# A fused attention and spectral-mixing kernel: v on the software DMA queue, a regrouped tail, and one SyncE transfer per stored pair

## The chip, the cores and the metric

The kernel runs on one core of a Trainium2 chip, in one launch. The metric is the device time in microseconds (us); medians are quoted. The record marks each run as fast or slow. All runs of kernels that were timed more than once are marked fast (none is over 1.5% above the fastest of its kernel); for the five single runs (e5 to e8 and e11) the state is unknown. A profile is one execution taken by the hardware profiler. Its span is about 2 us shorter than the time that is measured for the same execution (460.2 against 461.99 us for the kernel before).

PE is the matrix engine, PEld its weight loads, DVE the vector engine, ACT the scalar engine, POOL and SP (SyncE) the two engines that issue the DMA transfers here. Transfers from POOL go to the software DMA queue (q0), those from SyncE to the hardware queue (q1). Sixteen DMA engines serve both. Every operation is recorded through one helper, so all profile lines carry its line number, L37, and are told apart by the names of their tiles.

## The reference, cut to what matters

```python
# q, k, v: [8, 8, 576, 64] f32; w_phi: [64, 128]
# moe_w_r, moe_w_i: [64, 512, 512] f32 (134 MB together); moe_w_ch: [512, 512]
q_p, k_p = phi(q), phi(k)                 # t = x @ w_phi - max|x @ w_phi|; exp(t), exp(-t)
x = (q_p @ (k_p^T v)) / (q_p @ sum(k_p))  # heads side by side: [8, 576, 512]
X = rfft(x, axis=1)[:, :64]               # 64 modes
Y = per mode, complex: X[:, m] @ (w_r[m] + i w_i[m])
u = x + irfft(Y, n=576)
out = u + relu(u @ moe_w_ch)              # [8, 576, 512] f32, 9.44 MB
```

The kernel makes the attention per pair of batches and pair of heads, while the 64 weight tiles of the modes (2 MB of f32 each in HBM, cast to bf16 on the way) stream in behind. As the inverse transform and the product with `w_ch` are both linear, it keeps the mixed modes Y ("y") and Y @ w_ch ("z") and adds the inverse transform of y to x, and that of z to x @ w_ch. A "mix" is the product of modes with one weight tile. yst and zst are the tiles that hold the y and z of the modes just mixed, and yT is yst transposed. The first 48 modes are "absorbed" into x and x @ w_ch before the last weights are there; the other 16 ("late") are added in the tail, chunk by chunk, where the relu, the last sum and the store of the output follow.

## The kernel before

These are the parts that the change and the argument touch. A chunk is 128 rows of the output in SBUF: chunks 0 to 7 of a batch pair come in pairs (n, n + 1). In a pair's output tile, partition 64a + p holds rows 9p + 4a + c and 9p + 4a + c + 1 of one batch. Chunk 8 holds one row in nine of both batches.

```python
def load_v(self):
    self.vn = pin.tile([128, 2, 9, D_], F32, name="vn")
    load(self.vn, v, self.g, self.bp, sp)              # SyncE
...
class Absorb:                                          # y and z of one chunk
    def sums(self):
        r = slice(0, 96)
        self.p, self.q = bank(), bank()                # two PSUM banks
        back(self.p, self.n, self.bp, CI, yall, r)
        pe.matmul(self.q, lhsT=ident_b, rhs=xw[:, self.bp, self.n, :], ...)
        back(self.q, self.n, self.bp, CI, zall, r)
    def keep_x(self): ...                              # DVE: x += p
    def keep_w(self): ...                              # ACT: xw = q
...
# after each mix of the last group of weights (cut): the serial chain
    dve.tensor_tensor(out=yst, in0=py, in1=yacc[:, o, :], op=ALU.add)
    put(yst, o, yall, (0, 2))
    ...                                                # 4 transposes
    act.copy(yT, pt)
    ...                                                # 4 matmuls of 512 columns
    act.copy(zst, pz)
    put(zst, o, zall, (1, 3))
    # three absorbs (ab[-3], ab[-2], ab[-1]) lie between these steps at the very end
...
class Last:                                            # the tail, a pair of chunks
    def store(self):
        rows = [out[2 * bp + i].rearrange("(p c) e -> p c e", c=9) for i in range(2)]
        if n == 8:
            ...                                        # two halves: (sp, pool)
        o = pw.tile([128, 2, DMODEL], F32, name="of", tag="wt")
        dve.tensor_tensor(out=o, in0=self.pp, in1=self.rl, op=ALU.add)
        i, c = n // 4, n % 4
        for a in range(2):
            (sp, pool)[a].dma_start(
                rows[i][:, 4 * a + c:4 * a + c + 2, :], o[64 * a:64 * a + 64])
```

## Time and profile before

| | before |
|---|---|
| time, median of 3 runs | 462.84 us (461.55 to 462.95) |
| span of the profiled run | 460.2 us |
| HBM read, written | 163.64 MB, 9.44 MB |
| last mix begins | 416.42 us |
| first store issued | 426.27 us |
| stores | 40 transfers of 64 partitions, 20 from SyncE, 20 from POOL |

These two rows of the page cut the span into 40 slices of 11.5 us: the mean busy share of the 16 DMA engines (in tenths, 9 is 90% or more), and what they moved.

```profile
DMA  8999999999999999999999999999999999992897
GB/s 192 207 216 220 230 229 209 228 229 207 229 230 209 228 229 227 209 230 229 207 229 228 207 207 207 206 208 207 207 213 218 214 211 211 205 178 55 249 323 252
```

The DMA engines are busy from the second slice to the 36th, that is until about 414 us, then idle for one slice, then busy again with the stores. Everything up to the gap is paced by the loads, most of which are weights.

In the windows view each row is a stretch of time: its length, the busy us of each engine with the number of instructions, the granted clock of PE (1.00 is full speed), the DMA share and the GB/s moved. A share above 1 means that packets overlap.

```profile
core 0: us, PE busy (x) PEld busy (x) DVE busy (x) ACT busy (x) POOL busy (x), PEclk, DMA share, GB/s
...
400.00:410.00 10.00, 9.87 (x55) 3.63 (x56) 7.06 (x11) 6.59 (x12) 0.00 (x0) 1.00 1.37 206
410.00:414.00 4.00, 4.00 (x25) 1.65 (x25) 3.02 (x6) 2.85 (x5) 0.00 (x0) 1.00 0.80 133
414.00:417.00 3.00, 1.33 (x12) 0.49 (x10) 1.04 (x2) 1.24 (x3) 0.00 (x0) 1.00 0.22 36
...
428.00:440.00 12.00, 12.00 (x68) 3.59 (x65) 9.87 (x10) 8.58 (x16) 4.78 (x9) 1.00 0.97 315
440.00:452.00 12.00, 10.51 (x61) 3.17 (x60) 10.35 (x10) 7.92 (x15) 4.76 (x9) 1.00 0.92 304
```

The timeline (start, duration, engine, operation, count, idle time before it and what ended that) shows the chain between:

```profile
416.42 0.67 PE L37 MATMUL pt<-wt,XT 128*32 128x512 bf16 x8 [1.67 <-DMA wt<-in_moe_w_i_dram]
...
417.13 0.69 DVE L37 TENSOR_TENSOR yst<-pt,yacc 128x512 bf16<-128x512 f32 x1 [2.09 <-PE pt L37]
...
420.13 0.58 ACT L37 CAST zst<-pt 128x512 bf16<-128x512 f32 x1 [0.68 <-ACT xw L37]
...
425.01 1.23 DVE L37 TENSOR_TENSOR of<-pp,rl 128x1024 f32<-128x1024 f32 x1 [3.90 <-PE pp L37]
...
426.27 5.25 SPq L37 DMA_DIRECT2D out_dram<-of  x4
...
451.04 0.68 DVE L37 TENSOR_TENSOR ofr<-pp,rl 128x512 f32<-128x512 f32 x1
...
454.95 1.67 SPq L37 DMA_DIRECT2D out_dram<-ofr  x1
```

PE waits 1.67 us for the last weight tile. Its product goes through yst, the transposes, zst and the first sums to the first pair add (425.01), and the first store goes out at 426.27. The last store leaves SyncE at 454.95, although DVE had finished it at 451.72: SyncE's queue is behind. The DMA view lists the transfers of v and of the output: issuing engine, count, KB each, median us from issue to landing.

```profile
vn<-in_v_dram SPq DMA_DIRECT2D x16, 576.0 KB, 7.8
...
out_dram<-of SPq DMA_DIRECT2D x16, 256.0 KB, 4.9
out_dram<-of POOLq DMA_DIRECT2D x16, 256.0 KB, 5.0
...
out_dram<-ofr SPq DMA_DIRECT2D x4, 128.0 KB, 5.0
out_dram<-ofr POOLq DMA_DIRECT2D x4, 128.0 KB, 4.8
```

`of` is the output tile of a pair, `ofr` that of chunk 8.

### The profile page before, as it was taken

How to read it: one execution, taken by the hardware profiler on the slowest of the kernel's cores; microseconds unless marked ns; L12 is line 12 of the kernel's file. 1: busy time of each engine (PE TensorE's matmuls, PEld its weight loads, DVE VectorE, ACT ScalarE, POOL GpSimd, SP SyncE). 2: the span in 40 equal slices, each digit the busy share in tenths (PEclk: the TensorE clock that was granted, in tenths of full speed). 3: DMA queues.
4: the chain of work that ended last, by engine and by line, in shares of the span. 5: the costliest groups of instructions: out<-in, count | busy, mean ns of one | idle time of the engine just before them, and what ended most of it. 6: DMA issues, size and time to landing. Idle time of an engine off the chain costs nothing.

```text
span 460.2 us, 9716 instructions
## 1 busy us (share of the span) xinstructions
PE 331.6 (72%) x4041; PEld 207.1 (45%) x4084; DVE 270.0 (59%) x488; ACT 281.6 (61%) x475; POOL 92.4 (20%) x130
## 2 busy tenths in 40 slices
PE   1586767768767767877866776059997756997991
PEld 1365546546555545655654554024443322332330
DVE  6656676556677658568647784643331213773882
ACT  3696879676889769579758762214452322664771
POOL 6232112113111211222110115002121210000331
PEclk9998999797999999789879999559998987999997
DMA  8999999999999999999999999999999999992897
GB/s 192 207 216 220 230 229 209 228 229 207 229 230 209 228 229 227 209 230 229 207 229 228 207 207 207 206 208 207 207 213 218 214 211 211 205 178 55 249 323 252
DMA packets 86301, 99.27 MB, mean 216 GB/s; under 512 B 2800, under 2 KB 79728, under 8 KB 86256
## 3 DMA queue, kind: packets, MB, share of 16 engines
q0 software_dynamic: 77264, 81.80, 103.8%
q1 hardware_dynamic: 8992, 16.85, 12.0%
q8 instruction: 32, 0.52, 0.4%
q14 instruction: 13, 0.11, 0.1%
HBM read 163.64 MB, written 9.44 MB: 376 GB/s over the span
## 4 chain that ended last, share of the span: by engine, by line
issue 27%; PE 23%; ACT 15%; DMA 15%; DVE 13%; POOL 5%; POOLq 0%; ACTq 0%
PE one L37 9%; PE pt L37 8%; DMA wt<-in_moe_w_i_dram 7%; PE two L37 6%; DVE m L37 6%; DMA kb<-in_k_dram 6%; ACT AB L37 5%; ACT AQ L37 5%; DVE mk L37 2%; POOL wt L37 2%; POOL out_dram L37 2%; DMA qb<-in_q_dram 2%; DVE zall L37 2%; ACT kT L37 2%; ACT XT L37 1%
## 5 line engine op out<-in xcount | busy, mean ns | idle before, releaser
L37 ACT CAST xw<-pt 128x512 bf16<-128x512 f32 x72 | 42.0, 586 | 61.7 <-PE pt L37 60.5
L37 ACT ACTIVATE AB<-two 128x1024 bf16<-128x1024 f32 x64 | 62.8, 1051 | 6.2 <-DVE mk L37 3.8
L37 ACT ACTIVATE AQ<-two 128x1024 bf16<-128x1024 f32 x64 | 63.0, 1053 | 1.9 <-PE two L37 1.8
L37 PE MATMUL pt<-wchb,xT 128*128 128x512 bf16 x135 | 39.8, 412 | 20.0 <-DVE xT L37 19.7
L37 DVE TENSOR_REDUCE m<-two 128x8 f32<-128x1024 f32 x32 | 39.2, 1224 | 17.8 <-PE two L37 17.7
L37 DVE TENSOR_REDUCE mk<-two 128x8 f32<-128x1024 f32 x32 | 39.0, 1221 | 16.7 <-PE two L37 16.3
L37 POOL DMA_DIRECT2D wt<-in_moe_w_r_dram x30 | 26.3, 878 | 95.7 <-PE one L37 52.9
L37 POOL DMA_DIRECT2D wt<-in_moe_w_i_dram x28 | 24.5, 876 | 91.0 <-PE pt L37 46.1
L37 DVE TENSOR_TENSOR va<-vn,ee 128x1152 bf16<-128x1152 f32 x32 | 42.0, 1356 | 0.0
L37 DVE RECIPROCAL rd<-one 128x6 f32<-128x6 f32 x48 | 9.4, 195 | 51.5 <-PE one L37 51.5
L37 ACT COPY kT<-one 128x512 bf16<-128x512 bf16 (+1 forms) x32 | 19.2, 640 | 28.7 <-PE one L37 28.7
L37 DVE TENSOR_TENSOR xs<-pt,xs 128x512 bf16<-128x512 f32 x36 | 24.3, 691 | 19.0 <-PE pt L37 18.6
L37 PEld LDWEIGHTS <-minus 96*128 96x128 bf16 x288 | 26.3, 110 | 19.0 <-issue 13.4
L37 PEld LDWEIGHTS <-XT 128*32 128x32 bf16 x512 | 17.9, 180 | 34.2 <-issue 21.6
L37 PE MATMUL two<-w2blk,qT 128*128 128x256 bf16 x128 | 20.4, 285 | 17.6 <-ACT AB L37 12.9
L37 DVE COPY xT<-pt 128x512 bf16<-128x512 bf16 x36 | 15.1, 422 | 30.3 <-PE pt L37 30.3
L37 PE MATMUL two<-mT,minus 96*128 96x128 bf16 x256 | 29.3, 245 | 3.1 <-issue 1.9
L37 PEld LDWEIGHTS <-xs 128*128 128x128 bf16 x304 | 24.7, 100 | 15.2 <-issue 8.1
L37 POOL DMA_DIRECT2D kb<-in_k_dram x16 | 11.5, 716 | 95.5 <-PE one L37 94.7
L37 PEld LDWEIGHTS <-qT 128*128 128x128 bf16 x144 | 14.1, 101 | 32.5 <-issue 29.9
L37 PE MATMUL one<-kvz,AQ 128*128 128x65 bf16 x512 | 28.0, 211 | 0.0
L37 DVE TENSOR_TENSOR xs<-one,rd 128x384 bf16<-128x384 f32 x48 | 26.8, 558 | 1.6
(113 smaller groups left out, 673.9 us busy)
## 6 DMA issues: line engine op xcount, KB each, us to landing
wt<-in_moe_w_r_dram POOLq DMA_DIRECT2D x30, 1024.0 KB, 28.1
wt<-in_moe_w_i_dram POOLq DMA_DIRECT2D x28, 1024.0 KB, 28.6
vn<-in_v_dram SPq DMA_DIRECT2D x16, 576.0 KB, 7.8
kb<-in_k_dram POOLq DMA_DIRECT2D x16, 288.0 KB, 22.3
qb<-in_q_dram POOLq DMA_DIRECT2D x16, 288.0 KB, 22.1
out_dram<-of SPq DMA_DIRECT2D x16, 256.0 KB, 4.9
out_dram<-of POOLq DMA_DIRECT2D x16, 256.0 KB, 5.0
xs<-in_moe_w_i_dram POOLq DMA_DIRECT2D x2, 1024.0 KB, 26.9
```

Of the source, the lines that this page charges most:

```text
L37: ins = f(*args, **kwargs)
```

## The change: its intent, and the diff

The change means to shorten the tail and to free the hardware queue. v is loaded from POOL. In the tail, the first two chunks are finished one by one in PSUM banks of their own; for the first four chunks the absorbing of y goes ahead of that of z; yst, yT, z's product and zst are made in halves shared between DVE and ACT; all absorbs are done before the last mix. Each stored pair goes out in one SyncE transfer in place of two of 64 partitions. Cut to its core:

```diff
-            load(self.vn, v, self.g, self.bp, sp)
+            load(self.vn, v, self.g, self.bp, pool)
...
-    todo += [c.all for c in ab[:-3]]
+    todo += [c.only_x for c in ab[:4]] + [c.only_w for c in ab[:4]] + [c.all for c in ab[4:]]
...
-            dve.tensor_tensor(out=yst, in0=py, in1=yacc[:, o, :], op=ALU.add)
+            for h in range(2):
+                dve.tensor_tensor(out=yst[:, H * h:H * h + H], in0=py[:, H * h:H * h + H],
+                                  in1=yacc[:, o, H * h:H * h + H], op=ALU.add)
...
-            act.copy(zst, pz)
+            act.copy(zst[:, 0:H], pz[0])
+            dve.tensor_copy(zst[:, H:], pz[1])
...
-            for a in range(2):
-                (sp, pool)[a].dma_start(
-                    rows[i][:, 4 * a + c:4 * a + c + 2, :], o[64 * a:64 * a + 64])
+            rows = out[2 * bp + n // 4]
+            sp.dma_start(
+                bass.AP(tensor=rows.tensor, offset=rows.offset + n % 4 * DMODEL,
+                        ap=[[4 * DMODEL, 2], [9 * DMODEL, 64], [1, w * DMODEL]]),
+                o.rearrange("p a e -> p (a e)") if w > 1 else o)
...
     seq = [Last(bp, ns) for bp in range(NP) for ns in ((0, 1), (2, 3), (4, 5), (6, 7), (8,))]
+    seq[0:1] = [Last(0, (0,)), Last(0, (1,))]
```

The list `ap` gives [step, count] per dimension of the output side, slowest first: 2 x 64 x (512w), w being 2 for a pair and 1 for the first two chunks. The two outer dimensions cannot be merged, as 64 steps of 9 rows are not one step of 4 rows. The SBUF side of the same transfer counts 128 partitions. Chunk 8 is also stored in one SyncE transfer, but there 128 partitions stand against 128 equally spaced rows.

More of the change, by code (lines that the diff above doesn't have):

```diff
@@ L543, with banks @@
     ps2_cm.__exit__(None, None, None)
-    pst_cm = tc.tile_pool(name="pst", bufs=8, space=bass.MemoryType.PSUM)
-    pst = pst_cm.__enter__()
+    pst = ctx.enter_context(tc.tile_pool(name="pst", bufs=4, space=bass.MemoryType.PSUM))
+    pst2 = ctx.enter_context(tc.tile_pool(name="pst2", bufs=2, space=bass.MemoryType.PSUM))
     def bank(shape=(128, DMODEL), dt=F32):
         return pst.tile(list(shape), dt, name="pt", tag="pt")
+    def banks(dt=F32):
+        return pst2.tile([128, 2, DMODEL * (1 if dt == F32 else 2)], dt, name="pp", tag="pp")
     pb_cm = tc.tile_pool(name="pb", bufs=2)
@@ L557 @@
     CL = pb.tile([128, 5, 128], BF16, name="CL", bufs=1)
-    CM = pb.tile([128, 4, 128], BF16, name="CM", bufs=1)
+    CM = CF.rearrange("p c r m -> p (c r m)")[:, 0:1024].rearrange(
+        "p (i c s) -> p i c s", i=2, c=4)
     def inverse_tables():
@@ L595, in inverse_tables @@
         last = calc(calc(tm, 4.0, jm), 1.0, 56.0)
-        b0 = calc(b0, 0.0, 1.0, ALU.is_equal, ALU.mult)
-        for dst, m, r, only in ((CI, mode, r, None), (CL, late, r, None), (CM, last, rm, b0)):
+        b0, b1 = (calc(b0, float(i), 1.0, ALU.is_equal, ALU.mult) for i in range(2))
+        for dst, m, r, only in ((CI, mode, r, None), (CL, late, r, None), (CM[:, 0], last, rm, b0),
+                                (CM[:, 1], last, rm, b1)):
             n = 512 if only is not None else 640
@@ L650, in __init__, with sum_p, sum_q @@
             self.bp, self.n = bp, n
-        def sums(self):
-            r = slice(0, 96)
-            self.p, self.q = bank(), bank()
-            back(self.p, self.n, self.bp, CI, yall, r)
-            pe.matmul(self.q, lhsT=ident_b, rhs=xw[:, self.bp, self.n, :],
-                      start=True, stop=False)
-            back(self.q, self.n, self.bp, CI, zall, r)
+        def sum_p(self, p):
+            self.p = p
+            back(p, self.n, self.bp, CI, yall, slice(0, 96))
+        def sum_q(self, q):
+            self.q = q
+            pe.matmul(q, lhsT=ident_b, rhs=xw[:, self.bp, self.n, :], start=True, stop=False)
+            back(q, self.n, self.bp, CI, zall, slice(0, 96))
         def keep_x(self):
@@ L666, in keep_w, with only_x, only_w @@
             act.copy(xw[:, self.bp, self.n, :], self.q)
-        def all(self):
-            self.sums()
+        def only_x(self):
+            self.sum_p(bank())
+            self.keep_x()
+        def only_w(self):
+            self.sum_q(bank())
+            self.keep_w()
+        def all(self):
+            if chunks.index((self.bp, self.n)) % 2:
+                p, q = bank(), bank()
+            else:
+                t = banks()
+                p, q = t[:, 0], t[:, 1]
+            self.sum_p(p)
+            self.sum_q(q)
             self.keep_x()
@@ L686 @@
     ab = [Absorb(*c) for c in chunks]
-    todo += [c.all for c in ab[:-3]]
+    todo += [c.only_x for c in ab[:4]] + [c.only_w for c in ab[:4]] + [c.all for c in ab[4:]]
+    A = len(ab) + 4
     def fill(n):
@@ L699, in put @@
                 r = 32 * s + 16 * (o - 6)
-                sp.dma_start(yl[r:r + 16], src)
+                (sp, pool)[s // 2 if o == 7 else 0].dma_start(yl[r:r + 16], src)
     todo = [inverse_tables] + todo
-    while mixq:
-        key = mixq.pop(0)
-        g, o, i = key[0], key[1] // 2, key[1] % 2
-        if key not in wts:
-            next_w(1)
-        mix(*key, wts.pop(key), XTb[g % 2], bank)
-        next_w(1)
-        left = len(mixq)
-        n = -(-max(len(todo) - 33, 0) // (left - 7)) if left > 7 else -(-len(todo) // max(left, 1))
-        if g == NG - 1 and i == 1:
-            py = pys.pop(o)
-            yst = pb.tile([128, DMODEL], BF16, name="yst")
-            dve.tensor_tensor(out=yst, in0=py, in1=yacc[:, o, :], op=ALU.add)
-            put(yst, o, yall, (0, 2))
-            end = left == 0
-            if end:
-                ab[-3].sums()
-                ab[-3].keep_x()
-            fill(min(n, 1))
-            pt = bank([128, 4, 128], BF16)
-            for dc in range(4):
-                pe.transpose(pt[:, dc, :], yst[:, dc * 128:(dc + 1) * 128], ident_b)
-            yT = pb.tile([128, 4, 128], BF16, name="yT")
-            act.copy(yT, pt)
-            if end:
-                ab[-2].sums()
-                ab[-2].keep_x()
-                ab[-3].keep_w()
-            fill(min(n - 1, 1))
-            pz = bank()
-            for dc in range(4):
-                pe.matmul(
-                    pz, lhsT=yT[:, dc, :], rhs=wchb[:, dc, :],
-                    start=(dc == 0), stop=(dc == 3))
-            zst = pb.tile([128, DMODEL], BF16, name="zst")
-            act.copy(zst, pz)
-            put(zst, o, zall, (1, 3))
-            if end:
-                ab[-2].keep_w()
-                ab[-1].all()
-            fill(max(n - 2, 0))
-        else:
-            fill(n)
-    assert not todo
-    pst_cm.__exit__(None, None, None)
-    pst1 = ctx.enter_context(tc.tile_pool(name="pst1", bufs=4, space=bass.MemoryType.PSUM))
-    pst2 = ctx.enter_context(tc.tile_pool(name="pst2", bufs=2, space=bass.MemoryType.PSUM))
     class Last:
@@ L754, in __init__ @@
             self.bp, self.ns = bp, ns
-            self.early = bp == 0 and ns[0] < 4
+            self.early = bp == 0 and ns[0] < 6
+            self.first = bp == 0 and ns[0] < 2
         def base(self, which):
-            if which:
-                self.q = [pst1.tile([128, DMODEL], F32, name="qq", tag="qq") for _ in self.ns]
+            if self.first:
+                if which:
+                    self.pp = banks()
+                    self.q, self.p = [self.pp[:, 1]], [self.pp[:, 0]]
+            elif which:
+                self.q = [bank() for _ in self.ns]
             else:
-                self.pp = pst2.tile([128, 2, DMODEL], F32, name="pp", tag="pp")
+                self.pp = banks()
                 self.p = [self.pp[:, a] for a in range(len(self.ns))]
@@ L779, in straight, with keep_p @@
                 for a, n in enumerate(self.ns):
-                    pe.matmul((self.q if which else self.p)[a], lhsT=CM[:, n],
+                    pe.matmul((self.q if which else self.p)[a], lhsT=CM[:, n // 4, n % 4],
                               rhs=(yst, zst)[which], start=False, stop=True)
+        def keep_p(self):
+            self.rl = pb.tile([128, 2, DMODEL], F32, name="rl")
+            act.copy(self.rl[:, 0], self.p[0])
         def relu(self):
@@ L788, in store @@
         def store(self):
-            bp, n = self.bp, self.ns[0]
-            rows = [out[2 * bp + i].rearrange("(p c) e -> p c e", c=9) for i in range(2)]
+            bp, n, w = self.bp, self.ns[0], len(self.ns)
+            if w == 1:
+                o = pw.tile([128, DMODEL], F32, name="ofr", tag="wt")
+            else:
+                o = pw.tile([128, 2, DMODEL], F32, name="of", tag="wt")
+            if n == 0 and self.first:
+                dve.scalar_tensor_tensor(out=o, in0=self.q[0], scalar=0.0, in1=self.rl[:, 0],
+                                         op0=ALU.max, op1=ALU.add)
+            elif w == 1:
+                dve.tensor_tensor(out=o, in0=self.p[0], in1=self.rl[:, 0], op=ALU.add)
+            else:
+                dve.tensor_tensor(out=o, in0=self.pp, in1=self.rl, op=ALU.add)
@@ L791, in store @@
             if n == 8:
-                o = pw.tile([128, DMODEL], F32, name="ofr", tag="wt")
-                dve.tensor_tensor(out=o, in0=self.pp[:, 0], in1=self.rl[:, 0], op=ALU.add)
-                for i in range(2):
-                    (sp, pool)[i].dma_start(rows[i][:, 8, :], o[64 * i:64 * i + 64, :])
+                sp.dma_start(
+                    out[2 * bp:2 * bp + 2].rearrange("i (p c) e -> (i p) c e", c=9)[:, 8, :], o)
                 return
-            o = pw.tile([128, 2, DMODEL], F32, name="of", tag="wt")
@@ L798, in store @@
-            dve.tensor_tensor(out=o, in0=self.pp, in1=self.rl, op=ALU.add)
-            i, c = n // 4, n % 4
-            for a in range(2):
-                (sp, pool)[a].dma_start(
-                    rows[i][:, 4 * a + c:4 * a + c + 2, :], o[64 * a:64 * a + 64])
-    seq = [Last(bp, ns) for bp in range(NP) for ns in ((0, 1), (2, 3), (4, 5), (6, 7), (8,))]
-    seq[0].base(1)
-    seq[0].late(1)
+            rows = out[2 * bp + n // 4]
+            sp.dma_start(
+                bass.AP(tensor=rows.tensor, offset=rows.offset + n % 4 * DMODEL,
+                        ap=[[4 * DMODEL, 2], [9 * DMODEL, 64], [1, w * DMODEL]]),
+                o.rearrange("p a e -> p (a e)") if w > 1 else o)
@@ new lines @@
+    seq = [Last(bp, ns) for bp in range(NP) for ns in ((0, 1), (2, 3), (4, 5), (6, 7), (8,))]
+    seq[0:1] = [Last(0, (0,)), Last(0, (1,))]
+    H = DMODEL // 2
+    while mixq:
+        key = mixq.pop(0)
+        g, o, i = key[0], key[1] // 2, key[1] % 2
+        if key not in wts:
+            next_w(1)
+        if not mixq:
+            assert not todo
+            seq[0].base(1)
+            seq[0].late(1)
+        mix(*key, wts.pop(key), XTb[g % 2], bank)
+        next_w(1)
+        left = len(mixq)
+        n = -(-max(len(todo) - A, 0) // (left - 7)) if left > 7 else -(-len(todo) // max(left, 1))
+        if g == NG - 1 and i == 1:
+            end = left == 0
+            if end:
+                seq[0].base(0)
+                seq[0].late(0)
+            py = pys.pop(o)
+            yst = pb.tile([128, DMODEL], BF16, name="yst")
+            pt = [bank([128, 2, 128], BF16) for h in range(2)]
+            yT = [pb.tile([128, 2, 128], BF16, name=f"yT{h}") for h in range(2)]
+            for h in range(2):
+                dve.tensor_tensor(out=yst[:, H * h:H * h + H], in0=py[:, H * h:H * h + H],
+                                  in1=yacc[:, o, H * h:H * h + H], op=ALU.add)
+            put(yst, o, yall, (0, 2))
+            if not end:
+                fill(min(n, 1))
+            for h in range(2):
+                for dc in range(2):
+                    pe.transpose(pt[h][:, dc, :],
+                                 yst[:, H * h + 128 * dc:H * h + 128 * dc + 128], ident_b)
+                if h:
+                    dve.tensor_copy(yT[h], pt[h])
+                else:
+                    act.copy(yT[h], pt[h])
+            if not end:
+                fill(min(n - 1, 1))
+            else:
+                seq[0].straight(0)
+                seq[0].keep_p()
+                seq[1].base(1)
+            pz = [bank([128, H]) for e in range(2)]
+            for h in range(2):
+                for e in range(2):
+                    for dc in range(2):
+                        pe.matmul(
+                            pz[e], lhsT=yT[h][:, dc, :],
+                            rhs=wchb[:, 2 * h + dc, H * e:H * e + H],
+                            start=(h == dc == 0), stop=(h == dc == 1))
+            zst = pb.tile([128, DMODEL], BF16, name="zst")
+            act.copy(zst[:, 0:H], pz[0])
+            dve.tensor_copy(zst[:, H:], pz[1])
+            put(zst, o, zall, (1, 3))
+            fill(max(n - 2, 0))
+        else:
+            fill(n)
@@ L807 @@
+    assert not todo
+    seq[1].late(1)
+    seq[1].base(0)
+    seq[1].late(0)
     seq[0].straight(1)
-    seq[0].relu()
+    seq[1].straight(0)
+    seq[1].straight(1)
+    seq[1].relu()
     for g, s in enumerate(seq):
-        t = seq[g + 1] if g + 1 < len(seq) else None
+        t = seq[g + 1] if 0 < g < len(seq) - 1 else None
         if t:
             t.base(1)
-        s.base(0)
+        if g > 1:
+            s.base(0)
         if t:
             t.late(1)
-        s.late(0)
-        s.straight(0)
+        if g > 1:
+            s.late(0)
+            s.straight(0)
```

## The prediction

> **What bounds the kernel now.** Up to about 416 us it is the load stream. The windows view shows a DMA share of about 1.2 (packets overlap) in every stretch from 20 to 400 us, at 206 to 233 GB/s moved; the timeline shows PE waiting 1.67 us for the last weight tile until 416.42. Then comes the tail, 44 us: a serial chain up to the first store at 426.27, then stores until 460. There the DMA share is 0.88 to 1.00 at about 290 to 380 GB/s, while DVE adds four pairs and a single in 6.7 us (2.36 MB, 352 GB/s): DVE and the DMA engines are about even.
>
> **What the change moves.**
>
> 1. v (16 x 576 KB) goes from the hardware to the software queue. The same bytes run on the same engines: the packet records give 106 ns for a 2,304-byte v packet, and 107 ns for a k or q packet that reads as much. POOL pays about 0.7 us more for each issue, but is queued about 28 us ahead (issue to landing of a weight tile): no bubble, last weight at 416 +-2 us.
>
> 2. Tail chain. Before: mix 416.42, yst 417.13, transposes 417.88, yT 418.37, product 419.01, zst 420.13, two xw casts 420.61 to 421.69, q sums 421.74, two relus to 424.15, pair add 425.01 to 426.24. After: halves shared by ACT and DVE (an estimate of 0.35 us each from 0.58 to 0.69 us for whole ones), no xw casts behind zst, and a one-chunk first store, at about 421: 5 us gained.
>
> 3. Stores. Before, each half pair is 64 partitions to 64 rows. After, one SyncE transfer has 128 partitions on one side, but 2 x 64 x 1024 on the output side (order of instructions): its slowest dimension counts 2. The Trainium skill, page "DMA: Bandwidth & Descriptors", section "Why a DMA increments its semaphore by 16 and not by 1", says that a transfer runs on the largest k <= 16 that divides the slowest dimensions of both sides: here 2. No transfer of this trace has so small an outer dimension, so nothing here tests it. The stores of chunk 8 (128 against 128) keep 16.
>
> Cost of step 3: a 4,096-byte store packet took a median of 159 ns in the tail, one of 2,048 bytes 84 ns. Each of two engines gets 15 pairs x 64 x 159 ns = 152.6 us, two singles x 64 x 84 ns = 10.8 us, and about 3 us of chunk 8: 166 us in place of 34. All of it is on the critical path.
>
> **Prediction.** 421 + 1 (issue) + 166 + 2 (receipt) = 590 us of span, and 2 us more as timed: 593 us, 8 in 10 between 575 and 625 (packets at the mean of about 196 ns that share and rate imply would give about 630). Chances: faster by over 2% 0.05, within 2% 0.07, slower by over 2% 0.88.
>
> **What would show it.** Step 1: PE's wait for the last weight ends near 416. Step 2: first store issued near 421. Step 3: in the tail a DMA share near 2/16 = 0.12 at about 51 GB/s; a store 10 us when alone, more from issue to landing; DVE and PE idle, waiting for output tiles.
>
> **What would make it wrong.** The transfer is spread over 16 engines after all: then about 455 us, the gain of the chain. Two engines alone may run packets at another rate. v waiting in order on POOL could starve the weights.

## More of the kernel before

From 400 to 414 us PE is busy almost without a break. From 414 to 417 it idles for more than half of the time. In the store stage the DMA engines and PE are close to full, and DVE is busy for over 80%.

## The result, and the profile after

| | before | after |
|---|---|---|
| time, median of 4 runs | 462.19 us | 588.13 us (586.86 to 589.52) |
| span of the profiled run | 460.2 us | 587.7 us |
| last mix begins | 416.42 us | 415.95 us |
| first store issued | 426.27 us | 421.14 us |

The ratio after to before is 1.2727 (95% interval 1.2683 to 1.277). A ratio is the mean time of one kernel's runs over that of the other's of the same rounds, so not quite the ratio of the medians quoted. The changed kernel is 27% slower, as predicted (593, with 575 to 625).

The same two rows of the page, now in slices of 14.7 us:

```profile
DMA  9999999999999999999999999999211111111111
GB/s 175 227 207 228 228 213 228 241 207 228 228 228 228 227 228 227 227 225 206 204 207 202 207 216 219 215 205 191 50 54 68 52 53 68 53 52 69 53 69 45
```

Until the 28th slice (411 us) the picture is as before. Then 12 slices at a DMA share of a tenth or two and 45 to 69 GB/s follow, where before there were three at 250 to 320. The windows view:

```profile
400.00:410.00 10.00, 10.00 (x57) 3.96 (x57) 7.64 (x13) 6.26 (x12) 0.00 (x0) 1.00 1.29 195
410.00:414.00 4.00, 4.00 (x24) 1.65 (x23) 3.33 (x6) 2.53 (x6) 0.00 (x0) 1.00 0.36 61
414.00:417.00 3.00, 3.00 (x19) 0.95 (x17) 2.00 (x4) 2.05 (x4) 0.00 (x0) 1.00 0.00 0
...
428.00:440.00 12.00, 8.28 (x45) 2.42 (x45) 4.91 (x5) 4.94 (x10) 0.00 (x0) 0.97 0.14 54
440.00:452.00 12.00, 2.52 (x8) 0.49 (x8) 1.23 (x1) 1.08 (x2) 0.00 (x0) 0.50 0.13 53
...
500.00:560.00 60.00, 5.20 (x16) 0.95 (x15) 5.49 (x5) 2.77 (x5) 0.00 (x0) 0.50 0.14 57
```

In the store stage the share is 0.13 to 0.14, near 2/16 = 0.125, at 53 to 57 GB/s. PE and DVE, nearly full before, have little to do: they wait for output tiles to become free. The granted clock of 0.50 there is no rival cause: PE is busy for only 5.20 of 60 us. At the front, the loads are over by 414 us (share 0.00 from 414 to 417), and PE is busy all the time from 400 to 417. The timeline of the same stretch:

```profile
415.95 0.69 PE L37 MATMUL pt<-wt,XT 128*32 128x512 bf16 x8
...
416.70 0.76 DVE L37 TENSOR_TENSOR yst<-pt,yacc 128x256 bf16<-128x256 f32 x2 [0.98 <-PE pt L37]
...
420.42 0.69 DVE L37 SCALAR_TENSOR_TENSOR ofr<-pp,rl 128x512 f32<-128x512 f32 x1 [0.80 <-PE pp L37]
...
421.14 1.59 SPq L37 DMA_DIRECT2D out_dram<-ofr  x2
...
444.27 1.23 DVE L37 TENSOR_TENSOR of<-pp,rl 128x1024 f32<-128x1024 f32 x1 [8.71 <-DMA out_dram<-of]
...
562.06 3.89 SPq L37 DMA_DIRECT2D out_dram<-ofr  x1
```

The last mix starts without a wait for a weight. The first store leaves at 421.14, 5.13 us earlier than before. Then, at 444.27, DVE has waited 8.71 us for a store to land, and most adds behind it wait for one too. The view of the output tensor gives the time that SyncE spends on one issue (ns: minimum/median/maximum), here before, then after:

```profile
L37 SPq DMA_DIRECT2D out_dram<-of x16: 466/630/1759, 426.3 to 453.2; - x16
L37 POOL DMA_DIRECT2D out_dram<-of x16: 523/526/545, 426.5 to 451.4; - x16
```

```profile
L37 SPq DMA_DIRECT2D out_dram<-of x15: 751/9227/15927, 425.2 to 552.7; - x15
L37 SPq DMA_DIRECT2D out_dram<-ofr x6: 532/6774/17053, 421.1 to 562.1; - x6
```

A SyncE issue, 630 ns in the median before, takes 9,227 ns. What SyncE waits for inside an issue the trace does not name. The chain of waits points to the stores too. Its shares of the span, after:

```profile
by line: DMA out_dram<-of 15.8%; PE pt L37 2.8%; DMA out_dram<-ofr 2.6%; PE pp L37 2.2%; DVE ofr L37 0.1%; issue 0.0%; DVEq L37 0.0%
```

This view covers only 398 to 536 us, so the shares do not add up to 100%. From 427 us to the last add all of it is waiting for stores to land, 108 us. The packet records say the same most directly. After, a 4,096-byte store packet takes 159 ns in the median and 159.1 in the mean, and for 150.4 us exactly two store packets are in flight, where before 14 to 17 were in flight for most of the stage. One engine that moves 4,096 bytes in 159 ns does 25.8 GB/s, and two do 51.5.

### The profile page after: what moved, and what is told of

Same layout as the page of the kernel before. It is cut to its first block, busy times and chain, and to the rows that moved or that the text cites. A ratio compares the mean times of both kernels' runs of the same rounds, so it can differ in the third digit from the quotient of the medians.

```text
span 587.7 us, 9829 instructions
## 1 busy us (share of the span) xinstructions
PE 346.8 (59%) x4120; PEld 210.8 (36%) x4120; DVE 277.8 (47%) x522; ACT 277.5 (47%) x476; POOL 94.6 (16%) x128
## 5 line engine op out<-in xcount | busy, mean ns | idle before, releaser
L37 ACT CAST xw<-pt 128x512 bf16<-128x512 f32 x56 | 32.9, 588 | 52.9 <-PE pt L37 52.8
L37 ACT ACTIVATE rl<-pt 128x512 f32<-128x512 f32 x34 | 18.7, 595 | 77.4 <-DVE of L37 55.7
L37 PE MATMUL pt<-wchb,xT 128*128 128x512 bf16 x144 | 40.4, 406 | 25.0 <-DVE xT L37 23.9
L37 PE MATMUL pp<-xs,ident_b 128*128 128x512 bf16 x36 | 15.1, 495 | 58.8 <-DVE of L37 44.5
L37 DVE TENSOR_TENSOR of<-pp,rl 128x1024 f32<-128x1024 f32 x15 | 18.1, 1222 | 66.3 <-DMA out_dram<-of 61.1
L37 PEld LDWEIGHTS <-ident_b 128*128 128x128 bf16 x108 | 10.0, 105 | 65.2 <-issue 60.6
L37 PE MATMUL two<-qT,w2blk 128*128 128x512 bf16 x64 | 28.4, 444 | 6.7 <-ACT AQ L37 6.6
L37 PEld LDWEIGHTS <-xs 128*128 128x128 bf16 x304 | 24.3, 99 | 14.7 <-issue 7.7
```

Source lines behind the costliest of these rows:

```text
L37: ins = f(*args, **kwargs)
```

## The experiments

Twelve kernels were run, all with correct results. Those that ask about tens of us or more (e5 to e8 and e11) are single looks (one profile, one time, state unknown because a single run has none to compare with). The others are 6 fast runs each, beside 11 of the kernel before on the same chip. e1 to e4 shared one chip, e9 and e10 another, and e12 had a third, so across these groups it is the ratios to before that compare.

### e1_halves_sp: both halves again, still on SyncE alone

The change with this edit undone in shape, not in queue:

```diff
-            sp.dma_start(bass.AP(..., ap=[[4 * DMODEL, 2], [9 * DMODEL, 64], [1, w * DMODEL]]), o)
+            for a in range(2):
+                sp.dma_start(
+                    bass.AP(..., offset=rows.offset + (n % 4 + 4 * a) * DMODEL,
+                            ap=[[9 * DMODEL, 64], [1, w * DMODEL]]), of[64 * a:64 * a + 64])
```

> The changed kernel, but each 128-row store goes as two 64-row transfers, both from SyncE: one dimension of 64 on each side. Theory (the count of the slowest dimension sets how many DMA engines a transfer uses): 16 engines again, first store still near 421, all stores in about 31 to 34 us, 454 to 458 us timed. Rival (one SyncE queue cannot carry what two queues carried): it stays far above 500 us. Rival (the new tail or v on the software queue cost the time): it stays near 588 us.

Measured: 460.61 us (459.45 to 462.83), ratio to before 0.9982 (0.9954 to 1.0011). The 128 us are gone, with one SyncE queue, the new tail and v on POOL all kept: both rivals fall. But the expected 454 to 458 us was missed; the kernel is no faster than before. That miss is followed up below (e3, e4, e9, e12). In its profile the DMA share of the store stage is 0.90, where the changed kernel had 0.14:

```profile
428.00:440.00 12.00, 12.00 (x68) 3.53 (x67) 10.45 (x10) 8.53 (x17) 0.00 (x0) 1.00 0.90 286
```

### e5_cut_62, e6_cut_57, e7_cut_48: the count alone

To separate the count of the slowest dimension from everything else, each half was cut into two transfers at row 62, 57 or 48. All three kernels have the same number of plain SyncE transfers with one dimension for rows, to the same addresses; only the counts differ (62 + 2, 57 + 7, 48 + 16).

```diff
+            for a in range(2):
+                for lo, hi in ((0, 62), (62, 64)):        # or 57, or 48
+                    sp.dma_start(bass.AP(..., ap=[[9 * DMODEL, hi - lo], [1, w * DMODEL]]),
+                                 of[64 * a + lo:64 * a + hi])
```

> The changed kernel, but each half of a 128-row store goes as two SyncE transfers, of 62 and 2 rows. Theory: the largest k up to 16 that divides 62 is 2, and 2 for the rest, so again two engines move all: 580 to 600 us, DMA share near 0.13 in the tail. Rival (the extra dimension on the output side, or having 128 rows in one transfer, is slow, not the count): these are plain 62-row transfers, so near 470 us as e7_cut_48.

> As e5_cut_62, but cut at 57 and 7 rows. Theory: 57 rows run on 3 engines, 7 rows on 7. Engines 0 to 2 then carry about 97 + 5 + 3 us of packets at 159 ns each: 525 to 540 us. Rival: as e7_cut_48, near 470 us.

> As e5_cut_62, but cut at 48 and 16 rows: the same number of transfers, and 16 engines each. Theory: about 68 issues on SyncE at 0.55 to 0.65 us bound the stores: 462 to 475 us. If many transfers as such were slow, it would be as slow as e5_cut_62.

Measured: 589.09, 527.95 and 465.14 us. One row of the windows view of each (428 to 450 us), in this order:

```profile
428.00:450.00 22.00, 9.97 (x48) 2.63 (x47) 5.48 (x5) 5.93 (x11) 0.00 (x0) 0.73 0.13 53
```

```profile
428.00:450.00 22.00, 11.74 (x54) 2.79 (x52) 7.77 (x7) 6.76 (x13) 0.00 (x0) 0.70 0.27 95
```

```profile
428.00:450.00 22.00, 18.27 (x102) 5.33 (x100) 16.49 (x15) 13.53 (x25) 0.00 (x0) 1.00 0.86 232
```

The share (last but one) goes from 0.13 to 0.27 to 0.86, and the GB/s from 53 to 95 to 232. In the packet records two store packets were in flight for about 149 us of e5's stores, and three for about 68 us of e6's. All three times lie in the ranges expected. Cutting at 62 or at 48 is the same program but for the cut, and makes a difference of 124 us; e6 lies where 57 rows on three engines put it. So it is the count of the slowest dimension, and neither the second output dimension nor the 128 rows in one transfer. The Trainium skill, page "DMA: Bandwidth & Descriptors", section "Why a DMA increments its semaphore by 16 and not by 1", states this rule, and this case agrees with it at four counts: 2 x 64 (588.13 us), 62 (589.09), 57 (527.95), and multiples of 16 (460.61 to 465.14).

### e8_before_pair: the store alone, in the kernel before

```diff
-            for a in range(2):
-                (sp, pool)[a].dma_start(
-                    rows[i][:, 4 * a + c:4 * a + c + 2, :], o[64 * a:64 * a + 64])
+            sp.dma_start(bass.AP(..., ap=[[4 * DMODEL, 2], [9 * DMODEL, 64], [1, 2 * DMODEL]]),
+                         o.rearrange("p a e -> p (a e)"))
```

> The kernel before, with only its pair stores joined into one SyncE transfer of 2 x 64 rows. Theory: two engines, 16 pairs x 64 packets x 159 ns = 163 us after a first store at 426: 592 to 602 us. Rival (the new tail is what is slow): near 462 us.

Measured: 594.27 us, in the range expected. The old tail, the old queue for v and chunk 8 in halves leave it as slow. The part that costs the time needs none of the others.

### e11_pair_pool: the same 2 x 64 transfer from POOL

```diff
-            sp.dma_start(
+            pool.dma_start(
```

> The changed kernel with the whole 2 x 64 row store issued from POOL in place of SyncE. The Trainium skill's page on DMA says that the software queue gives a transfer of k = 2 two consecutive engines from a cursor that moves on. Then several stores in flight lie on different engines: six output tiles in flight, 12 engines, a store about 10 us: 465 to 490 us, with a DMA share of 0.5 to 0.8 in the tail. If POOL's stores too keep to the same two engines: near 588 us. If the software queue spreads them over 16: 456 to 460 us.

Measured: 508.73 us, which lies between the cases and outside the range expected for any of them. From 428 to 450 us:

```profile
428.00:450.00 22.00, 8.98 (x47) 2.58 (x48) 5.51 (x6) 5.54 (x10) 3.94 (x5) 0.77 0.67 153
```

The share is 0.67 here, five times that of SyncE, and later falls: the packet records have from 2 to 14 store packets in flight, two of them for 16 us. POOL's issue stayed at 0.79 us, so POOL never waited, but a pair store took 23.9 us in the median to land, not 10, and DVE stood still for 14.5 us once. So stores from POOL do not all share the same two engines, as those from SyncE do. That fits the sentence of the page, in the section named above, that the software queue moves on from engine to engine; but the trace does not number the engines, so that the waits come from stores which landed on engines in use is only an inference. I had expected six tiles in flight to keep 12 engines busy.

### e2_halves_sp_v_sync and e4_before_v_pool: v alone

e2 is e1 with v back on SyncE; e4 is the kernel before with v on POOL, and nothing else.

```diff
-            load(self.vn, v, self.g, self.bp, sp)
+            load(self.vn, v, self.g, self.bp, pool)      # e4, on the kernel before; e2 undoes it on e1
```

> As e1_halves_sp, but v goes back to the SyncE queue. Theory: v's packets cost less time on the software queue (4,608 bytes in 178 ns against twice 106 ns, 4.0 us per engine over the kernel), so here the last weight lands 2 to 4 us later and the kernel is 1 to 3 us slower than e1_halves_sp. Rival: the queue does not matter, or PE hides it: within 0.7 us.

> The kernel before, with v on the software queue alone. Theory: the 1.67 us for which PE waited for the last weight goes, and the load stream ends 2 to 4 us earlier: 1.5 to 3 us faster than before. Rival: no effect, within 0.7 us of before; or slower, if v waiting in order on POOL starves the weights.

Measured: e2 465.55 us, ratio to before 1.0073 (1.004 to 1.0106), against e1's 0.9982: taking v off POOL costs 0.9%, about 4 us. e4 459.0 us, ratio 0.9941 (0.9916 to 0.9967): about 3 us faster than before. So v's move is a gain by itself, in both tails. In the new tail it is larger than the 1 to 3 us expected. e2 also shows the change without v's move and with its stores on 16 engines: it is 0.7% slower than before, clear of noise.

The packet records show one cause that I had overlooked. On the hardware queue v moved in 4,096 packets of 2,304 bytes at a mean of 106.4 ns, 27.2 us on each of the 16 engines. On the software queue it moved in 2,048 packets of 4,608 bytes at a mean of 181.3 ns (after), 23.2 us on each: 4.0 us less in a stage where the DMA engines are the limit. The last weight packet ended at 416.10 us before, at 413.79 after and at 412.53 in e4. POOL did wait in order for a free v tile, 35.4 us in all in the changed kernel, but DVE waited only 2.9 us for v, and the DMA share stayed at 1.2: the queue ahead was deep enough.

The timeline of e4 around the last mix:

```profile
413.58 0.69 DVE L37 TENSOR_TENSOR yst<-pt,yacc 128x512 bf16<-128x512 f32 x1 [2.10 <-PE pt L37]
```

Its idle time before yst is 2.10 us, as in the kernel before: with the old distribution of absorbs PE still waits for the last weight, and the whole of the earlier landing reaches the tail. One half of e4's theory thus fell: PE's wait for the last weight did not go (1.67 us again), it only ended earlier.

### e3_halves_sp_pool, e9_balanced, e10_pool_halves: which queue carries the halves

e3 sends the halves of a pair from SyncE and POOL, as the kernel before did. e9 does so for chunk 8 as well. e10 sends all from POOL.

```diff
-            sp.dma_start(bass.AP(..., ap=[[4 * DMODEL, 2], [9 * DMODEL, 64], [1, w * DMODEL]]), o)
+            for a in range(2):
+                (sp, pool)[a].dma_start(               # e10: (pool, pool)
+                    bass.AP(..., ap=[[9 * DMODEL, 64], [1, w * DMODEL]]), of[64 * a:64 * a + 64])
```

> As e1_halves_sp, but the second half of each pair goes from POOL, as in the kernel before. Theory: DMA engines and DVE bound the stores, so within 1.5 us of e1_halves_sp. Rival: SyncE's issue time holds e1 back: this is 2 to 5 us faster.

> As e3_halves_sp_pool, but chunk 8 too goes as one half from SyncE and one from POOL, as in the kernel before. In e3 POOL's last store packet ended at 452.2 and SyncE's at 456.3, with a SyncE issue taking up to 2.1 us. Theory (SyncE's queue holds more bytes and drains last): balanced, both end near 454.5: 1 to 2.5 us faster than e3, 456.5 to 458 us. Rival (the bytes as such bound the stores): within 0.7 us of e3.

> As e9_balanced, but every half goes from POOL, whose issues took 0.53 us each whatever the queue held. 36 halves at 0.53 us fit beside DVE's 1.29 us per pair. Theory (a SyncE issue is what backs up): 456 to 459 us. Rival (one queue of either kind carries less than two): as e1_halves_sp, 460 to 462 us.

Measured: e3 459.08 us, ratio 0.9936 (0.9909 to 0.9962). e9 458.57 us, ratio 0.9922 (0.9898 to 0.9945). e10 462.27 us, ratio 0.9997 (0.997 to 1.0024).

e3 against e1 is 1.5 us by the medians, on the border between its theory and its rival. SyncE's issues do back up in both. In e3:

```profile
L37 SPq DMA_DIRECT2D out_dram<-of x15: 466/839/2123, 422.5 to 450.4; - x15
L37 POOL DMA_DIRECT2D out_dram<-of x15: 528/531/548, 422.8 to 446.5; - x15
```

Beside POOL's even 531 ns, a SyncE issue took up to 2,123 ns. e9 did what its mechanism said (POOL's last store packet ended at 454.28 and SyncE's at 455.23, where in e3 they were 4 us apart), and from the first store to the end of the last store packet it took 34.5 us in place of 37.9. But it missed the 456.5 to 458 us expected, and the gain over e3 is not resolved by these intervals. e10's theory fell: a POOL issue never grew, and the kernel was still 3.7 us slower than e9. Slow stores are not what its profile shows: their share is 0.91 to 1.01 from 430 to 454 us, and from the first store to the last packet they took 34.9 us, against e9's 34.5. The 4.3 us between the two profiles lie mostly before the first store (2.3 us, with the last mix 2 us later) and after the last packet (3.4 us to the end in place of 1.8). So that one queue carries less than two is not shown; why the kernel is slower is left open.

e9 has the lowest median, 0.8% below before. It beats both kernels of the change. Against e4, which has the old tail, it gains nothing that the intervals show.

### e12_defer: fewer absorbs before the last mix

In the profiles of after, e9 and e10 PE is busy without a break from 400 us to the last mix. (In e1 and e3 it is not: there the last mix began 0.33 us after the last weight packet had ended, about as in the kernel before.) e12 is e9 with the last five chunks not absorbed; their early modes are added in the tail.

```diff
-    todo += [...] + [c.all for c in ab[4:]]
+    todo += [...] + [c.all for c in ab[4:-5]]
...
+                if (self.bp, n) in chunks[-5:]:
+                    back((self.q if which else self.p)[a], n, self.bp, CI,
+                         zall if which else yall, slice(0, 96), False, True)
```

> As e9_balanced, but the last five chunks are not absorbed before the last mix: their early-mode matmuls join the sums of the tail (3 matmuls, a DVE add and an ACT cast less each before the last mix, 2 matmuls more each behind it). In e9 PE was 100% busy from 400 us to the last mix, which came about 3 us after the last weight; in the tail the stores drain for 7 us after DVE's last add. Theory (PE's absorbing, not the load stream, now sets the last mix): yst starts 2 to 3 us earlier, near 413.6 to 414.5, the tail is as long, and the kernel takes 455.5 to 457.5 us. Rival (the load stream sets it, or the added tail matmuls cost as much): within 0.7 us of e9, 458 to 459.5 us.

Measured: 459.54 us (457.28 to 460.61), ratio 0.9941 (0.9913 to 0.9969). No gain; the theory as stated fell. In its profile yst starts at 415.17, 1.15 us earlier than in e9's, while the last weight packet had ended at 413.18. PE was still nearly full from 405 us to the last mix (8.90 of 9 us up to 414): the code spreads the remaining absorbs evenly over the last weights, so work taken out of the end is taken from all of them. That this is why PE stayed full is not shown: PE's granted clock was also 0.77 from 405 to 410 us here and 1.00 in e9. A single profile cannot carry 2 us here. Nine kernels (after, e1, e3, e5, e6, e7, e9, e10, e11) have the same code up to the last mix, and in their profiles yst starts between 414.04 and 418.31 us.

## Why the prediction was right

**The store.** Right, and for the reason given. Two engines move every pair: two packets in flight, share 0.13 to 0.14, 159 ns per 4,096 bytes. From the first issue to the end of the last store packet it is 165 us in place of 32 (586.0 - 421.1 after, 458.6 - 426.3 before), against a predicted 166 and 34. The prediction took the median packet, 159 ns, in place of the mean of the crowded stage before (196 ns by share and rate). That turned out right (with two engines the mean is 159.1 ns), but the prediction gave no reason for it and named 630 us for the other choice, so in this term it had some luck. The slower mean before goes with 14 to 17 packets in flight at once; what slows them there no run separates.

**The first store.** Right: 421.14 for 421. The place in time depends on the last mix, which varies (next paragraph). The chain itself, from yst to the first store, took 4.44 us in place of 9.14, so 4.7 us were gained where 5 were predicted. The halves cost 0.38 us each for yst (0.76 for two), 0.37 and 0.29 for yT, 0.37 and 0.42 for zst, where 0.35 was estimated.

**The last weight.** The prediction said that "the same bytes run on the same engines" and expected no change. That step failed. The packet size differs by queue, and so does the time: 4.0 us less per engine. The last weight packet ended 2.3 us earlier than before. PE's last mix nevertheless started at 415.95, near the predicted 416, because in this profile PE was still busy with other work, three more absorbs among it, for 2.2 us after that packet. So the number was met for another reason, and by luck: in the eight other profiles with the same code up to there the last mix began between 413.31 and 417.58 us. Its delay behind the last weight packet goes with the clock that PE was granted from 380 to 400 us: 0.3 us where that was 0.88 and 0.92 (e1, e3), 0.8 to 0.9 us at 0.86 (e6, e7), and 1.5 to 3.8 us at 0.83 (after, e5, e9, e10, e11). With the old tail it was 0.3 us at 0.83 too (before, e8). This fits a PE that has more to do before the last mix and falls behind at a lower clock, but no run sets the clock and the profiles come from several chips, so it is not shown.

**What would be left with 16 engines.** The prediction said "about 455 us, the gain of the chain". That was wrong: e1 took 460.61 and e3 459.08, and v's move accounts for the whole of e3's gain (e4: 459.0 with the old tail). The step that failed is to count the earlier first store as an earlier end. In e3 the first store left at 418.47, 4.2 us before e4's (422.71), but DVE's last add came only 1.3 us earlier, at 446.15 against 447.49:

```profile
414.04 0.76 DVE L37 TENSOR_TENSOR yst<-pt,yacc 128x256 bf16<-128x256 f32 x2 [1.07 <-PE pt L37]
...
417.75 0.69 DVE L37 SCALAR_TENSOR_TENSOR ofr<-pp,rl 128x512 f32<-128x512 f32 x1 [0.80 <-PE pp L37]
...
421.26 1.23 DVE L37 TENSOR_TENSOR of<-pp,rl 128x1024 f32<-128x1024 f32 x1 [1.75 <-PE pp L37]
...
446.15 0.68 DVE L37 TENSOR_TENSOR ofr<-pp,rl 128x512 f32<-128x512 f32 x1
```

```profile
413.58 0.69 DVE L37 TENSOR_TENSOR yst<-pt,yacc 128x512 bf16<-128x512 f32 x1 [2.10 <-PE pt L37]
...
421.46 1.23 DVE L37 TENSOR_TENSOR of<-pp,rl 128x1024 f32<-128x1024 f32 x1 [3.90 <-PE pp L37]
423.62 3.85 DVE L37 TENSOR_TENSOR of<-pp,rl 128x1024 f32<-128x1024 f32 x3 [0.94 <-ACT rl L37]
...
447.49 0.68 DVE L37 TENSOR_TENSOR ofr<-pp,rl 128x512 f32<-128x512 f32 x1
```

In e3 the add at 421.26 is that of chunks 2 and 3, behind two single chunks; e4 begins that one at 423.62. So e3 is 2.4 us ahead there, and 1.3 us of it are left at the last add. That the early start is not worth more fits engines that are full behind it: PE is busy for all 12 us of 428 to 440 in both.

```profile
428.00:440.00 12.00, 12.00 (x69) 3.59 (x68) 10.54 (x10) 8.52 (x16) 3.93 (x8) 1.00 0.94 296
```

```profile
428.00:440.00 12.00, 12.00 (x71) 3.61 (x69) 9.89 (x10) 9.16 (x18) 4.70 (x10) 1.00 0.98 333
```

The tail is 36 chunks of PE and DVE work, and it ends when that work ends and its stores have drained. From the start of yst to that of the last add it took 33.9 us with the old tail (before and e4) and 32.1 with the new one (e3 and e9), so the chain's 4.7 us had shrunk to 1.8. The three absorbs moved ahead of the last mix could account for these, but then they stand on PE before it; no run moves them alone. e2's profile fits that side, with v on SyncE and the last weight landing as before: yst at 419.16 where before had 417.13. In e3 the stores also drained at 296 GB/s from 428 to 440 us, where e4 did 333, and from the start of the last add to the end of the last store packet it took 10.2 us, where e4 took 6.9. SyncE had been given chunk 8 as a whole; e9, which shared it out, took 6.8, but its yst began at 416.32 and e4's at 413.58. How much of the remaining difference between e9 and e4 is real is not settled by these runs.

## What to carry to other kernels

Before joining two transfers into one, look at the count of the slowest dimension on both sides as the instruction will carry it: 128 partitions against 2 x 64 rows ran on two DMA engines, and a 62-row transfer did too, while 64 and 48 rows ran on sixteen. A share of k/16 in the profile of a stage that should be full, with packets at their usual time, is the sign of it. And an earlier first result is only worth what the stage behind it can use: where PE and DVE are full to the end, ask how much work is left, not when it starts.

## What the Trainium skill lacked or had wrong

- "DMA: Bandwidth & Descriptors", section "Rules for kernel authors", says of two transfers to disjoint partition halves "Don't bother" and advises one 128-partition transfer. Here the one transfer took the kernel to 588.13 us and the two halves to 460.61 us, because the output side's slowest dimension counted 2. The same table has the rule on outer dimensions below 16 elsewhere; the two should name each other.
- The same table says that spreading transfers over queues does not help bandwidth and only saves issue time. The runs do not show this to be wrong. e9 (both queues) took 458.57 us and e10 (POOL alone) 462.27, but in their profiles the stores took 34.5 and 34.9 us, and in e3 (both) and e1 (SyncE alone) 37.9 and 38.0.
- The page does not say that a SyncE issue grows when its transfers run on few engines: 0.47 us at the least, 0.63 us in the median before, 9.23 us in the median when two engines carried everything. POOL's issue of a half stayed between 0.52 and 0.56 us in before, e3 and e10, and that of 2 x 64 rows at about 0.8 in e11.
- No page says that the two queues cut the same load into packets differently: v came in packets of 2,304 bytes (106.4 ns) from SyncE and of 4,608 bytes (181.3 ns) from POOL, 4.0 us less per engine over the kernel.
- The page's account of the software queue (k = 2 takes two engines that move on) was not enough to foresee e11: with up to six tiles in flight, 2 to 14 packets were, and the kernel took 508.73 us.
